# Start addresses of the MLP operands within 64 bytes, and one unread product ahead of the MLP's long run

## The chip, the cores and the metric

The kernel runs on one core of a Trainium2 chip. The metric is the device time of one execution in microseconds (us), lower is better. Three runs of the kernel before took 1395.46, 1397.22 and 1397.25 us, median 1397.22.

## The reference

Attention with mixed heads, and two MLPs behind it, all in float32. q, k and v are 4 x 12 x 448 x 64 (batch, heads, positions, width), the model width is 768, the inner width of both MLPs 2048:

```
scores = einsum('bhij,hg->bgij', q @ k^T / 8, w_pre)
attn   = softmax(scores)
attn   = einsum('bhij,hg->bgij', attn, w_post)
x      = (attn @ v), heads side by side            # 1792 x 768
x      = elu(x @ w_in) @ w_out                     # first MLP
out    = relu(x @ w_in2)**2 @ w_out2               # second MLP
```

## The kernel before

Every float32 operand of the scores, the pre mix and the MLPs is split into a high and a low part of type fp32r, and a product is three matmuls: high x high, high x low, low x high. In the MLPs the helper `three` issues them (lines 576 to 578). Its first two operands are the stationary ones, which a weight load brings into TensorE; the last two are the moving ones, which stream through it.

Attention runs in 90 steps of two row groups each. In a step come two pre mixes (lines 189 to 191, fp32r, 120 x 120 stationary, 448 columns moving), softmax, sometimes a set of scores (line 162) or of `values` (line 245, the product with v, in float32, 64 stationary columns, two halves of the array in turn), and then two post mixes (`mix_post`, line 220, float32, 112 stationary columns, 120 moving ones, two records on the engine for each matmul). Behind the last step the code calls `mlps.begin()`, which issues the first 36 MLP matmuls, and after it the last two `values`, which fill the wait for the last mixed rows. Then `run` issues the rest of the MLPs.

The 1792 rows go through the MLPs in two halves of 896, and each half in four stages:

- inner stage of the first MLP: 16 blocks of the inner width, two blocks of 448 rows, 6 steps of the sum, three matmuls each, 576 matmuls of 448 columns. Stationary is a weight (`wh`, `wl`), moving is `xh` or `xl`. In the first half the 36 of `begin` are part of it
- outer stage of the first MLP (w1o): 576 matmuls of 448 columns, stationary a weight, moving `hh` or `hl`
- inner stage of the second MLP: as the first
- outer stage of the second MLP (w2o): 672 matmuls of 384 columns. Here the roles change: stationary is `hh` or `hl`, moving is a weight

Each weight comes by a DMA as 64-bit numbers, is turned into float32 by one operation of ScalarE and four of VectorE (lines 430 to 454), and split (lines 467 and 468). The second half loads float32 weights that the first half kept.

Where the tiles lie: as built, within a partition, `xh` begins at byte 186336 and `xl` at 207840, the four buffers of `wh` at 148704 to 154848 and of `wl` at 156896 to 163040, all 32 bytes past a multiple of 64. `hh` and `hl` begin at 16512 and 73856, multiples of 64. All slices that `three` takes step by multiples of 256 bytes, so a stage has one start for each role:

| stage | stationary starts at (mod 64) | moving starts at (mod 64) |
|---|---|---|
| both inner stages | 32 | 32 |
| w1o | 32 | 0 |
| w2o | 0 | 32 |

Of the pre mix, `gh` and `gl` (moving) are at 0, `pre_l` at 0 and `pre_h` at 32. The tile `pre`, from which `pre_h` and `pre_l` are made, is at byte 16512, under what becomes `hh`.

The PSUM banks have three tags, `qk` with four buffers, `mix` and `post` with two each. The MLPs take them in the order mix, post, qk, qk (`Mlps.bank`).

Of the kernel before, what the change touches and what calls it, by code (L numbers as in the profile page):

```python
# [8 lines left out]
F32R = mybir.dt.float32r  # L9
# [6 lines left out]
B, H, S, D = 4, 12, 448, 64  # L16
# [4 lines left out]
JC, NJ = 4, 112  # L21
KC, FC = DM // 128, DFF // 128
WU = 512
EXP_MIN, EXP_MAX = 2.0**-15, float.fromhex("0x1.dffffep+16")


# [17 lines left out]
def bank(psum, tag):  # L44
    return psum.tile([128, 512], F32, name=f"ps_{tag}", tag=tag, bufs=BANKS[tag])


def attention(tc, psum, qr, kr, vr, w_pre, w_post, diagonal, xd, mlps):
    nc = tc.nc
    with ExitStack() as ctx:  # L50
# [339 lines left out]
        for i in range(2):  # L390
            values(N - 1, i)


class Weights:

# [5 lines left out]
    def __init__(self, nc, dram, layers):  # L401
        self.nc = nc
        self.units = []
        kept = [dram.tile([count, 128, n], F32, name=f"{name}f", tag=f"{name}f") for name, _, count, n in layers]
        for half in range(2):
            for k, (name, src, count, n) in zip(kept, layers):
                self.units += [(half, src[i], k[i], n) for i in range(count)]
        self.raw, self.single, self.parts, self.keep = {}, {}, {}, []
        self.loaded = self.sized = self.turned = self.done = self.used = 0

    def load(self, room=None):
        i = self.loaded
        self.loaded += 1
        half, src, kept, n = self.units[i]
        if half == 0:
            self.raw[i] = (room() if room else self.pool.tile([128, WU, 2], I32, name="wd", bufs=4))[:, :n, :]
            self.nc.sync.dma_start(out=self.raw[i].rearrange("p n t -> p (n t)"), in_=src.bitcast(I32))
        else:
            self.single[i] = self.pool.tile([128, WU], F32, name="wf", bufs=6)[:, :n]
            self.nc.sync.dma_start(out=self.single[i], in_=kept)  # L420

    def size(self, room=None):

        i = self.sized
        self.sized += 1
        half, src, kept, n = self.units[i]
        if half == 1:
            return
        f = (room() if room else self.pool.tile([128, WU], F32, name="wf", bufs=6))[:, :n]
        self.nc.scalar.activation(f, self.raw[i][:, :, 1].bitcast(F32), AF.Abs)  # L430
        self.single[i] = f
# [5 lines left out]
    def turn_op(self, k):  # L437

        nc = self.nc
        i = self.turned  # L440
        half, src, kept, n = self.units[i]
        if half == 0:
            if self.sized == i:
                self.size()
            t, f = self.raw[i], self.single[i]
            low, high, w = t[:, :, 0], t[:, :, 1], f.bitcast(I32)
            if k == 0:
                nc.vector.tensor_scalar(f, f, EXP_MIN, EXP_MAX, ALU.max, ALU.min)
            elif k == 1:
                nc.vector.tensor_scalar(w, w, 5, 2, ALU.logical_shift_left, ALU.logical_shift_right)  # L450
            elif k == 2:
                nc.vector.scalar_tensor_tensor(w, high, -0x40000000, w, ALU.bitwise_and, ALU.bitwise_or)
            else:
                nc.vector.scalar_tensor_tensor(w, low, 29, w, ALU.logical_shift_right, ALU.bitwise_or)  # L454
                del self.raw[i]
                self.keep.append((kept, f))
        self.turned += k == 3

    def part(self, engine=None):
        nc = self.nc  # L460
        i = self.done
        self.done += 1
        f = self.single.pop(i)
        n = self.units[i][3]
        hi = self.pool.tile([128, WU], F32R, name="wh", bufs=4)[:, :n]
        lo = self.pool.tile([128, WU], F32R, name="wl", bufs=4)[:, :n]
        nc.scalar.copy(hi, f)  # L467
        (engine or nc.vector).tensor_tensor(lo, f, hi.bitcast(F32), ALU.subtract)  # L468
        self.parts[i] = hi, lo
# [27 lines left out]
def col(i):  # L497
    return slice(i * 128, (i + 1) * 128)


class Mlps:
# [14 lines left out]
    def tmp(self):  # L516
        return self.tp.tile([128, S], F32, name="tmp", bufs=5)

    def two_parts(self, shape, pool, name):
        return [pool.tile(shape, F32R, name=f"{name}{a}", tag=f"{name}{a}") for a in "hl"]  # L520


    def plan(self, put, M, last, work, early, early_ctx, score_ctx):
# [29 lines left out]

    def new_x(self, half):
        self.half, self.xraw = half, {}
        self.nx = self.two_parts([128, KC, 2 * S], self.xp, "x")

    def piece(self, i):

# [37 lines left out]
    def run(self):  # L597
        nc, weights, blocks = self.nc, self.weights, self.blocks
        self.hp = self.pool("hp", "left")
        for half in range(2):  # L600
            xh, xl = self.nx
            for m in range(2):
                hh, hl = self.two_parts([128, FC, 2 * S], self.hp, "h")
                pending = []

                def activate(p, f, bl, m=m, hh=hh, hl=hl):
                    u = g = self.tmp()
                    if m == 0:
                        nc.scalar.activation(u, p, AF.Relu, scale=-1.0)
                        nc.scalar.activation(u, u, AF.Exp, scale=-1.0)  # L610
                        nc.vector.scalar_tensor_tensor(g, u, -1.0, p, ALU.add, ALU.max)
                    else:
                        nc.scalar.activation(u, p, AF.Relu)  # L613
                        nc.vector.tensor_tensor(g, u, u, ALU.mult)  # L614

                    def rest():
                        nc.scalar.copy(hh[:, f, bl], g)
                        nc.vector.tensor_tensor(hl[:, f, bl], g, hh[:, f, bl].bitcast(F32), ALU.subtract)

                    pending.append(rest)  # L620

                def flush():
                    for rest in pending:
                        rest()
                    pending.clear()

                for f in range(FC):
                    if half == m == f == 0:
                        p = self.begun
                    else:  # L630
                        p = self.inner(xh, xl, flush)
                    for j, bl in enumerate(blocks):
                        activate(p[j], f, bl)
                flush()
                if m == 0:
                    xh, xl = self.two_parts([128, KC, 2 * S], self.xp, "x")
                    for o in range(KC):
                        p = [self.bank()[:, :S] for _ in blocks]
                        for f4 in range(4):
                            wh, wl = weights.next()  # L640
                            for j, bl in enumerate(blocks):
                                for i in range(4):
                                    f = 4 * f4 + i
                                    self.three(p[j], wh[:, col(i)], wl[:, col(i)], hh[:, f, bl], hl[:, f, bl],
                                               f == 0, f == FC - 1)
                        for j, bl in enumerate(blocks):
                            nc.scalar.copy(xh[:, o, bl], p[j])
                            nc.vector.tensor_tensor(xl[:, o, bl], p[j], xh[:, o, bl].bitcast(F32), ALU.subtract)
                    continue
                n2 = DM // 2  # L650
                for nh in range(2):
                    p = [self.bank()[:, :n2] for _ in range(7)]
                    for f in range(FC):
                        if half == 0 and nh == 0:
                            if f == 0:
                                self.new_x(1)
                            if f < 12:
                                self.load_x(f)
                            if 2 <= f < 14:
                                self.split_x(f - 2)  # L660
                        wh, wl = weights.next()
                        for i in range(7):
                            self.three(p[i], hh[:, f, col(i)], hl[:, f, col(i)], wh[:, :n2], wl[:, :n2],
                                       f == 0, f == FC - 1)
                    for i in range(7):
                        o = self.tmp()[:, :n2]
                        if i % 2:
                            nc.scalar.copy(o, p[i])
                        else:
                            nc.vector.tensor_copy(o, p[i])  # L670
                        r = half * 2 * S + i * 128
                        nc.sync.dma_start(out=self.out[r : r + 128, nh * n2 : (nh + 1) * n2], in_=o)
# [49 lines left out]
```

## Time and profile before

| | us |
|---|---|
| median of three runs | 1397.22 |
| the profiled execution | 1395.56 |
| its span, first to last instruction | 1393.8 |
| attention, up to the first matmul behind the last values | 445.9 |
| MLPs from there to the last matmul's start | 944.1 |

The profile is one execution on the one core. TensorE has two rows, PE for the matmuls and PEld for the weight loads, which run beside them; DVE is VectorE, ACT ScalarE, POOL GpSimd. A matmul's record is longer than its share of the engine, since the next one starts before it ends: what counts is the pitch, from the start of one to the start of the next. Where the pitch is even, a record of an MLP matmul is some 161 to 164 ns longer than it.

### The profile page before, as it was taken

What the parts mean: (1) busy time and instruction counts of PE and PEld (TensorE: products, weight loads), DVE (VectorE), ACT (ScalarE), POOL (GpSimd) and SP (SyncE); (2) the same over time, 40 slices, a digit from 0 to 9 for tenths busy, and PEclk for the clock granted to TensorE, in tenths of its full rate; (3) what the DMA queues carried; (4) which work ended last, traced back from release to release, by engine and by line L of the source; (5) the groups of instructions that cost most, each with busy time, mean ns of one, the idle gap of its engine ahead of it and who ended that gap; (6) DMA issues with size and microseconds to landing.
All of it is one profiled execution on the core that took longest, in us unless ns stands there. A gap on an engine that the chain in (4) does not pass through costs nothing.

```text
span 1393.8 us, 24193 instructions
## 1 busy us (share of the span) xinstructions
PE 1381.4 (99%) x8906; PEld 1249.7 (90%) x8906; DVE 859.0 (62%) x1928; ACT 669.6 (48%) x1504; POOL 263.4 (19%) x245
## 2 busy tenths in 40 slices
PE   7999999999999999999999999999999999999999
PEld 4888888888889999999999999999999999999998
DVE  6877778777886989766688886534442114443121
ACT  5776767676775666322354543245541113333111
POOL 3755665665554000000000000000000000000000
PEclk9999999999999999999999999999999999999999
DMA  5624633734544555544455575431221111111131
GB/s 157 198 105 146 192 106 131 205 107 130 192 137 158 180 159 177 189 148 144 143 163 154 166 253 186 150 100 54 61 68 53 46 46 46 57 56 57 36 108 40
DMA packets 104810, 174.40 MB, mean 125 GB/s; under 512 B 22675, under 2 KB 82163, under 8 KB 104691
## 3 DMA queue, kind: packets, MB, share of 16 engines
q1 hardware_dynamic: 104691, 172.85, 39.4%
q8 instruction: 70, 1.15, 0.3%
q14 instruction: 49, 0.40, 0.1%
HBM read 97.93 MB, written 36.18 MB: 96 GB/s over the span
## 4 chain that ended last, share of the span: by engine, by line
PE 98%; DVE 1%; ACT 0%; DMA 0%; issue 0%; POOL 0%; SPq 0%; DVEq 0%
PE ps_post L220 12%; PE ps_qk L576 11%; PE ps_qk L577 11%; PE ps_qk L578 11%; PE ps_mix L577 6%; PE ps_post L577 6%; PE ps_mix L576 6%; PE ps_post L576 6%; PE ps_post L578 6%; PE ps_mix L578 6%; PE ps_qk L245 6%; PE ps_qk L162 4%; PE ps_mix L191 3%; PE ps_mix L190 2%; PE ps_mix L189 2%; DMA k_room<-kr 0%
## 5 line engine op out<-in xcount | busy, mean ns | idle before, releaser
L467 ACT CAST wh<-wf 128x384 fp32r<-128x384 f32 (+1 forms) x240 | 126.6, 532 | 272.4 <-DVE wf L454 113.8
L468 DVE TENSOR_TENSOR wl<-wf,wh 128x384 fp32r<-128x384 f32 (+1 forms) x238 | 137.3, 581 | 163.2 <-ACT wh L467 162.3
L183 POOL TENSOR_TENSOR gl<-graw,gh 120x448 fp32r<-120x448 f32 x178 | 201.5, 1154 | 145.7 <-ACT gh L178 142.4
L220 PEld LDWEIGHTS ps_post<-wg,ex 120*112 120x112 f32 x1440 | 156.1, 177 | 21.6 <-DVE tot L204 7.5
L220 PE MATMUL ps_post<-wg,ex 120*112 120x120 f32 x1440 | 172.9, 272 | 0.7 <-DVE at L227 0.6
L198 ACT ACTIVATE ex<-ps_mix,nmax 120x448 f32<-120x448 f32 x180 | 113.5, 637 | 113.5 <-DVE nmax L196 110.2
L576 PE MATMUL ps_qk<-xh,wh 128*128 128x448 f32 x384 | 141.4, 368 | 0.0
L577 PE MATMUL ps_qk<-xl,wh 128*128 128x448 f32 x384 | 141.3, 368 | 0.0
L578 PE MATMUL ps_qk<-xh,wl 128*128 128x448 f32 x384 | 141.3, 368 | 0.0
L196 DVE TENSOR_REDUCE nmax<-ps_mix 120x1 f32<-120x448 f32 x180 | 109.6, 622 | 41.7 <-PE ps_mix L191 41.3
L227 DVE COPY at<-ps_post 112x480 f32<-112x480 f32 x162 | 105.4, 650 | 9.9 <-PE ps_post L220 9.9
L178 ACT CAST gh<-graw 120x448 fp32r<-120x448 f32 x180 | 95.2, 593 | 0.1
L614 DVE TENSOR_TENSOR tmp<-tmp 128x448 f32<-128x448 f32 x64 | 39.9, 623 | 77.6 <-ACT tmp L613 77.6
L165 ACT COPY sc<-ps_qk 120x448 f32<-120x448 f32 x178 | 82.2, 558 | 7.1 <-PE ps_qk L162 7.0
L245 PEld LDWEIGHTS ps_qk<-at,v 112*64 112x64 f32 x1536 | 73.8, 137 | 11.3 <-ACT gh L178 6.5
L245 PE MATMUL ps_qk<-at,v 112*64 112x110 f32 (+2 forms) x1536 | 81.8, 262 | 0.0
L576 PEld LDWEIGHTS ps_qk<-xh,wh 128*128 128x128 f32 x384 | 72.1, 188 | 7.3
L577 PEld LDWEIGHTS ps_qk<-xl,wh 128*128 128x128 f32 x384 | 72.1, 188 | 7.3
L578 PEld LDWEIGHTS ps_qk<-xh,wl 128*128 128x128 f32 x384 | 72.1, 188 | 7.2
L430 ACT ACTIVATE wf<-wd 128x384 f32<-128x384 f32 (+1 forms) x120 | 69.4, 578 | 18.0 <-DMA wd<-w2o 8.6
L577 PE MATMUL ps_qk<-wl,hh 128*128 128x384 f32 x224 | 75.9, 339 | 0.0
L576 PE MATMUL ps_qk<-wh,hh 128*128 128x384 f32 x224 | 75.8, 339 | 0.0
(137 smaller groups left out, 3155.4 us busy)
## 6 DMA issues: line engine op xcount, KB each, us to landing
graw<-sc SPq DMA_DIRECT2D x180, 210.0 KB
wd<-w1i SPq DMA_DIRECT2D x32, 384.0 KB
wd<-w1o SPq DMA_DIRECT2D x24, 512.0 KB
wd<-w2i SPq DMA_DIRECT2D x32, 384.0 KB
wd<-w2o SPq DMA_DIRECT2D x32, 384.0 KB
w1if<-wf SPq DMA_DIRECT2D x32, 192.0 KB
w1of<-wf SPq DMA_DIRECT2D x24, 256.0 KB
w2if<-wf SPq DMA_DIRECT2D x32, 192.0 KB
```

The lines of the kernel that those rows point to most:

```text
L178: nc.scalar.copy(hi, graw[t])
L183: engine.tensor_tensor(lo, graw.pop(t), parts[t][0].bitcast(F32), ALU.subtract)
L196: nc.vector.tensor_reduce(nmax, p, AX.X, ALU.max, negate=True)
L198: nc.scalar.activation(e[-1], p, AF.Exp, bias=nmax, scale=1.0, accum_out=tot[:, t % 2 : t % 2 + 1])
L220: nc.tensor.matmul(p[:, c, :], e[:, c * NJ : (c + 1) * NJ], w, start=True, stop=True)
L227: nc.vector.tensor_copy(o, p)
L245: nc.tensor.matmul(p[64 * a : 64 * a + 64, k, :w], vt[b, i][:, jc, g * D : (g + 1) * D], at[n][:, jc, 6 * i + g, :w], start=(jc == 0), sto ...
L467: nc.scalar.copy(hi, f)
L468: (engine or nc.vector).tensor_tensor(lo, f, hi.bitcast(F32), ALU.subtract)
L576: mm(p, wh, xh, start=first, stop=False)
L577: mm(p, wh, xl, start=False, stop=False)
L578: mm(p, wl, xh, start=False, stop=last)
```

## The change

There are two parts.

1. Start addresses. The tiles of `xh`, `xl`, `hh` and `hl` become 16 elements (64 bytes) longer, and what is used of them begins `at` elements in: 8 (32 bytes) for x, 0 for the hidden values of the first MLP, 8 for those of the second. The weights of w2o begin 8 elements into their tiles, all others at 0 as before. Worked out from the tile sizes, the x pool grows down from the same top by 128 bytes, so `xh`'s tile stays at 32 past a multiple of 64 and its used part comes to a multiple of 64; the weight tiles move down by 128 bytes and stay at 32; `hh` stays at 16512 and `hl` comes to 73920. So in every stage of the MLPs the moving operands begin at a multiple of 64 bytes and the stationary ones 32 past one.
2. Behind the last `values` one more matmul is issued: the first 112 columns of `pre` stationary, all its 120 columns moving, float32, into a bank of tag `post`. Nothing reads the result.

```
+OFF = 8
         for i in range(2):
             values(N - 1, i)

+        flat = pre.rearrange("p r g -> p (r g)")
+        nc.tensor.matmul(bank(psum, "post")[:NJ, :120], flat[:, :NJ], flat, start=True, stop=True)
...
-                self.units += [(half, src[i], k[i], n) for i in range(count)]
+                self.units += [(half, src[i], k[i], n, name == "w2o") for i in range(count)]
...
-        hi = self.pool.tile([128, WU], F32R, name="wh", bufs=4)[:, :n]
-        lo = self.pool.tile([128, WU], F32R, name="wl", bufs=4)[:, :n]
+        at = OFF * self.units[i][4]
+        hi = self.pool.tile([128, WU], F32R, name="wh", bufs=4)[:, at : at + n]
+        lo = self.pool.tile([128, WU], F32R, name="wl", bufs=4)[:, at : at + n]
...
-    def two_parts(self, shape, pool, name):
-        return [pool.tile(shape, F32R, name=f"{name}{a}", tag=f"{name}{a}") for a in "hl"]
+    def two_parts(self, k, pool, name, at):
+
+        n = k * 2 * S
+        t = [pool.tile([128, n + 2 * OFF], F32R, name=f"{name}{a}", tag=f"{name}{a}") for a in "hl"]
+        return [x[:, at : at + n].rearrange("p (k s) -> p k s", k=k) for x in t]
...
-        self.nx = self.two_parts([128, KC, 2 * S], self.xp, "x")
+        self.nx = self.two_parts(KC, self.xp, "x", OFF)
...
-                hh, hl = self.two_parts([128, FC, 2 * S], self.hp, "h")
+                hh, hl = self.two_parts(FC, self.hp, "h", m * OFF)
...
-                    xh, xl = self.two_parts([128, KC, 2 * S], self.xp, "x")
+                    xh, xl = self.two_parts(KC, self.xp, "x", OFF)
```

## Rows read from the trace of the kernel before

**Rows 1.** The page: span, busy time of PE, the chain that ended last

```profile
span 1393.8 us, 24193 instructions
...
PE 1381.4 (99%) x8906; PEld 1249.7 (90%) x8906; DVE 859.0 (62%) x1928; ACT 669.6 (48%) x1504; POOL 263.4 (19%) x245
...
PE 98%; DVE 1%; ACT 0%; DMA 0%; issue 0%; POOL 0%; SPq 0%; DVEq 0%
```

**Rows 2.** Stretches, PE alone: start:end us, length, busy (records), clock, DMA

```profile
434.72:440.80 6.08, 6.08 (x32) 1.00 0.27 78
446.61:557.59 110.98, 110.98 (x538) 1.00 0.56 180
557.59:676.62 119.03, 119.03 (x577) 1.00 0.49 160
676.62:795.65 119.03, 119.03 (x577) 1.00 0.50 157
795.65:914.38 118.73, 118.73 (x674) 1.00 0.57 184
914.38:1033.41 119.03, 119.03 (x578) 1.00 0.24 72
```

**Rows 3.** Timeline of PE around the 36 early MLP matmuls: start us, us, what

```profile
431.26 0.97 PE L245 MATMUL ps_qk<-at,v 112*64 112x110 f32 x16
432.17 1.89 PE L220 MATMUL ps_post<-wg,ex 120*112 120x120 f32 x16
433.82 0.45 PE L576 MATMUL ps_mix<-xh,wh 128*128 128x448 f32 x1
434.11 0.36 PE L577 MATMUL ps_mix<-xl,wh 128*128 128x448 f32 x1
...
434.72 0.36 PE L577 MATMUL ps_mix<-xl,wh 128*128 128x448 f32 x1
...
440.80 0.36 PE L577 MATMUL ps_post<-xl,wh 128*128 128x448 f32 x1
```

**Rows 4.** Timeline of PE behind the last values

```profile
445.60 0.35 PE L245 MATMUL ps_qk<-at,v 112*64 112x108 f32 x4
445.89 0.47 PE L576 MATMUL ps_qk<-xh,wh 128*128 128x448 f32 x1
446.20 0.36 PE L577 MATMUL ps_qk<-xl,wh 128*128 128x448 f32 x1
446.40 0.37 PE L578 MATMUL ps_qk<-xh,wl 128*128 128x448 f32 x1
446.61 0.37 PE L576 MATMUL ps_qk<-xh,wh 128*128 128x448 f32 x1
```

**Rows 5.** Matmuls on tile hh: ns min/median/max, first and last start

```profile
L576 PE MATMUL ps_qk<-wh,hh x224: 336/338/342, 796.7 to 1389.7; 128*128 128x384 f32 x112
```

**Rows 6.** Timeline of PE, the last two pre mixes

```profile
427.09 0.36 PE L189 MATMUL ps_mix<-gh,pre_l 120*120 120x448 f32 x1
427.28 0.36 PE L190 MATMUL ps_mix<-gh,pre_h 120*120 120x448 f32 x1
427.48 0.37 PE L191 MATMUL ps_mix<-gl,pre_h 120*120 120x448 f32 x1
```

**Rows 7.** Timelines of DVE, PE and ACT: readers of the banks, first write of hh

```profile
434.10 0.53 DVE L229 COPY at<-ps_post 112x360 f32<-112x360 f32 x1 [0.29 <-PE ps_post L220]
...
448.68 0.61 DVE L611 SCALAR_TENSOR_TENSOR tmp<-tmp,ps_post 128x448 f32<-128x448 f32 x1
...
455.29 0.37 PE L576 MATMUL ps_post<-xh,wh 128*128 128x448 f32 x1
...
449.41 1.03 ACT L617 CAST hh<-tmp 128x448 fp32r<-128x448 f32 x2
```

**Rows 8.** Stretches, all engines: PE, PEld, DVE, ACT, POOL busy (records), clock, DMA

```profile
460.00:550.00 90.00, 90.00 (x437) 81.74 (x437) 83.01 (x176) 62.12 (x124) 0.00 (x0) 1.00 0.54 167
```

More of the change, by code (lines that the diff above doesn't have):

```diff
@@ L413, in load @@
         self.loaded += 1
-        half, src, kept, n = self.units[i]
+        half, src, kept, n, moves = self.units[i]
         if half == 0:
@@ L425, in size @@
         self.sized += 1
-        half, src, kept, n = self.units[i]
+        half, src, kept, n, moves = self.units[i]
         if half == 1:
@@ L440, in turn_op @@
         i = self.turned
-        half, src, kept, n = self.units[i]
+        half, src, kept, n, moves = self.units[i]
         if half == 0:
```

## The prediction

> **What bounds the kernel now.** I began with the busy times and the chain of waits on the page: TensorE's matmul row is busy 1381.4 of 1393.8 us, and 98% of the chain that ended last is its own matmuls [rows 1]. So no other engine, queue or transfer counts unless it starves TensorE. Next I cut the MLPs into their stages and asked for TensorE's busy time in each: it fills every stretch without a gap, at full granted clock, which of the two levels is 2.4 GHz [rows 2]. What is left to look at is how long a matmul occupies the engine, its pitch. The bounds of the stretches are starts of matmuls, so length over count is the pitch:
>
> - inner stage of the first half, from the fourth matmul behind the last values: 110.98 us / 537 = 206.67 ns [rows 2]
> - w1o: 119.03 / 576 = 206.65 ns, and the same for the next inner stage and for the first one of the second half [rows 2]
> - w2o, 384 columns: 118.73 / 672 = 176.68 ns [rows 2]
>
> Then I read the start of the MLPs one matmul at a time, because there the same matmuls stand behind two different neighbours. The 36 early ones follow a post mix. From the fifth to the thirty-fifth, 30 pitches, they take 6.08 us, 202.67 ns each [rows 2, 3]. Behind the last values the same kind of matmul, on the same tiles and weight buffers, falls within three matmuls to 206.67 and stays there for 537 in a row [rows 2, 4]. Operands, shapes, clock and addresses mod 64 are alike, so 4.0 ns a matmul hang on something that the engine carries over from what ran before it. It is carried far: w2o has another pitch for 672 matmuls, and the inner stage behind it is at 206.65 again [rows 2]. The trace shows that this is so, not what it is. I call the two the short and the long rhythm.
>
> **The change part by part.** *The unread product* puts something like a post mix where the values now lead straight into the long run. The trace has that order once: values until 432.17, post mixes, then the early matmuls in the short rhythm [rows 3]. There the post mix made 16 records; the new product makes 2. If two are enough, all 448-column matmuls behind it run at 202.67: 540 of the first inner stage less the 3 that lead in, 576 of the next two stages, 3 x 576 of the second half, say 3420. That is 3420 x (206.67 - 202.67) = 13.7 us saved, all of it on the chain, as TensorE has no gaps. For w2o, whose pitch in the short rhythm no row shows, I take no change; its records spread from 336 to 342 ns [rows 5], so single pitches lie about 3 ns on either side of the mean, and 1344 matmuls at 3 ns would be 4.0 us either way.
>
> The product itself costs its own time. Now the first MLP matmul starts behind the last values and the second 0.31 us later [rows 4]. With a product between, two records of some 0.10 to 0.19 us (16 in 1.89 us with the first wait in it) precede it, and the first fp32r matmul behind a post mix has a pitch of 0.29 instead of 0.31 [rows 3, 4]. I charge 0.2 us; 0 and 0.4 are the ends.
>
> What it could wait for: the bank of tag `post` that it takes was last read by the copy of the last mixed rows, at 434.10 to 434.63 [rows 7], 11 us before. What could wait for it: the tag's two buffers change parity, so the next MLP block on a `post` bank, at 455.29, now takes the buffer whose last reader ends at 449.29 [rows 7]; 6 us cover it. The tile `pre` lives until the product has read it, and `hh` lies over it, but the first write of `hh` is at 449.41, more than 3 us after the values that it waits for anyway [rows 7]; no more than 0.2 us could come back there, in ScalarE's queue, with the weights' casts behind it. I cost all three at nothing.
>
> *The start addresses* add no instruction, wait or byte of transfer; the moves of the pools by 128 bytes put no tile over a neighbour that it did not lie over before. They touch two of the four stages in what the engine sees as relative start: inner stages go from 32/32 (stationary/moving, mod 64) to 32/0, w2o from 0/32 to 32/0. w1o has 32/0 already, and there the pitch in the long rhythm is the same 206.65 as with 32/32 [rows 2]. So in the long rhythm the new addresses are worth nothing for 448 columns. In the short rhythm 32/0 is only seen in the pre mixes, which have loads of 120 columns and no more than six in a row: 0.19 and 0.20 us, about 196 and 200 ns [rows 6]. With loads of 128 columns it will be somewhat more. The nearest row in kind is the early stretch, 202.67, and I take it for the new addresses too, that is 0 for this part. Its ends: 196 as in the shortest pre mix, which is 6.7 x 3456 = 23 us more saved, and 206.67, which takes the whole gain back.
>
> Beside TensorE only VectorE comes near: in the first inner stage it is busy 83.0 of 90 us [rows 8], 92%. At 202.67 the stage is 2% shorter and VectorE at 94%; at 196 it would be 97%. So it starves nothing before the low end.
>
> The Trainium skill has a rule against the address part: TensorE: Matmul & The Clock Gate, Step-by-step: what each phase is for, says that the moving operand and the weight load have independent read ports, so that loading the next weights takes no read bandwidth from the running matmul. By it no start address would matter, and this part would be worth exactly nothing. The equal pitch of w1o and the inner stages agrees; the two rhythms of one and the same matmul are nothing that it explains.
>
> Sum against the profiled execution: 1395.6 - 13.7 + 0.2 = 1382.1 us. That execution is 1.7 us under the median of the runs shown, so against the median 1397.2 - 13.5 = 1383.7, say 1384.
>
> **The rivals.**
>
> *Nothing moves.* The long rhythm comes back at once, because two records don't do what 16 did, or because it hangs on the phase in which the first fp32r matmul happens to start; or the first change of stage brings it back (540 x 4.0 = 2.2 us saved). For it: the trace has only one start in the short rhythm, of 36 matmuls. Against it: within that stretch nothing drifts, and the long rhythm outlives three changes of stage. 1395 to 1397.5.
>
> *Lost half way.* The short rhythm holds in the first half and is lost at w2o: (540 + 1152) x 4.0 = 6.8 us, 1390.5. Against it speaks that the long rhythm outlives w2o.
>
> *The addresses bring more than the rhythm.* With 32/0 in the short rhythm the pitch goes to that of the shorter pre mixes: between 196 and 199.5 for 448 columns, and w2o to the lower edge of its records, 3 ns less. At 198: (206.67 - 198) x 3420 + 3 x 1344 + 0.2 = 29.7 + 4.0 = 34 us, 1363; at 196 it is 1357. For it: the pre mixes are the only rows with this pairing and have the lowest pitches. Against it: loads of 120 columns, runs of six.
>
> *Slower: w2o takes w1o's pairing and with it its evenness.* w1o, with 32/0, has one single pitch and it is the long one; w2o, with 0/32, varies, and only its longest matmuls reach 342 ns, 4 ns over the median of 338 [rows 5]. If the long rhythm stays and 32/0 makes each of the 1344 as long as the longest, w2o's pitch becomes about 180: 1344 x 3.3 = 4.5 us, with the product 1402. It decides from a rise of 2.1 ns in w2o's mean, if the other stages keep theirs.
>
> TensorE: Matmul & The Clock Gate, Back-to-back issue gap, in the Trainium skill gives a floor for a matmul by itself, columns / 2.4 GHz + 2.5 ns. An estimate from it: 189.2 ns for 448 columns and 162.5 for 384, 79 us in all, 1318; no stretch of the MLPs comes near it, and I give it 1 in 100, inside the chance of the rival that the addresses bring more.
>
> **How the numbers follow.** Chances: forecast 0.52 (1376 to 1389 with w2o's 4 us, the product's ends and 1 ns on the pitch); addresses bring more 0.15; lost half way 0.07; nothing moves 0.16; slower 0.10. A measurement of this kernel can tell 0.2%, 2.8 us, from no change. Forecast, the larger gain and the half-way case are faster: 0.74. Same: 0.16. Slower: 0.10. The range of 8 in 10 leaves out the slower case and about a third of the larger gain: 1360 to 1399.
>
> **What would show each step.** Right: a stretch of the first inner stage of the changed kernel has a pitch near 202.7 in uneven single pitches, w1o too, and the first inner stage of the second half still has it. The product shows as two records of line 220's kind of length behind the last values and TensorE has no gap after it. Wrong: an even 206.67 behind the product (two records are not enough, or the phase decides); a change of pitch in the inner stages but not in w1o, which has no new addresses (then it is the addresses, not the rhythm); w2o even at 180; or a pitch under 200 everywhere, by which the addresses would be worth more than the rhythm. A wait of TensorE for `wl` in the first inner stage would mean that VectorE has become the bound.

## The result, and the profile after

The changed kernel takes 1380.59 us (median of 4 runs, 1380.01 to 1381.63), the kernel before in the same comparison 1396.43 us. The ratio is 0.9888, 95% interval 0.9875 to 0.9900: 1.1% faster. The forecast was 1384 us, range 1360 to 1399. Size and direction came out; the cause that I gave for it did not, as the experiments show.

The page of the changed kernel answers to [rows 1]: TensorE is still busy all the time, only for less of it.

```profile
span 1378.3 us, 24196 instructions
...
PE 1366.5 (99%) x8908; PEld 1247.3 (90%) x8908; DVE 859.0 (62%) x1928; ACT 669.5 (49%) x1504; POOL 263.4 (19%) x245
...
PE 97%; DVE 1%; ACT 0%; issue 0%; DMA 0%; POOL 0%; SPq 0%; ACTq 0%; DVEq 0%; POOLq 0%
```

VectorE and ScalarE do the same work in the same busy time as before. The stretches of TensorE by stage (start:end us, length, busy and records, clock, DMA share, GB/s), which answer to [rows 2]; each runs from the start of a matmul to that of another:

```profile
446.90:556.09 109.19, 109.19 (x538) 1.00 0.57 182
556.09:673.21 117.12, 117.12 (x577) 1.00 0.51 163
673.21:790.33 117.12, 117.12 (x577) 1.00 0.50 159
790.33:906.83 116.50, 116.50 (x673) 1.00 0.58 188
906.83:1023.95 117.12, 117.12 (x577) 1.00 0.24 73
```

Length over matmuls: 109.19 / 537 and 117.12 / 576 are 203.33 ns in every 448-column stage, inner or w1o alike, where it was 206.67. 116.50 / 672 is 173.4 ns for w2o (the first few matmuls of it are longer; from the ninth on 173.33), where it was 176.68. The sum: 3420 x 3.33 ns = 11.4 us and 1344 x 3.33 ns = 4.5 us, less 0.3 us for the later start of the long run, 15.6 us. The two profiled executions differ by 1395.56 - 1380.11 = 15.5 us. So nothing is hidden elsewhere: the whole change is in the pitch.

The timeline of TensorE behind the last values (start us, us, what), answering to [rows 4]:

```profile
445.97 0.46 PE L395 MATMUL ps_post<-pre 120*112 120x120 f32 x2
446.19 0.45 PE L584 MATMUL ps_qk<-xh,wh 128*128 128x448 f32 x1
446.48 0.37 PE L585 MATMUL ps_qk<-xl,wh 128*128 128x448 f32 x1
446.68 0.38 PE L586 MATMUL ps_qk<-xh,wl 128*128 128x448 f32 x1
446.90 0.37 PE L584 MATMUL ps_qk<-xh,wh 128*128 128x448 f32 x1
```

The product is there with its two records. The first MLP matmul moves from 445.89 to 446.19; 0.22 us of that lie between the start of the product and it, the rest was there before the product.

One thing already spoke against my reading: the 36 early matmuls, which I took as the model for what a post mix does, ran at 202.67 ns before and run at 203.33 now. The fifth and the thirty-fifth of them:

```profile
434.77 0.37 PE L585 MATMUL ps_mix<-xl,wh 128*128 128x448 f32 x1
...
440.88 0.37 PE L585 MATMUL ps_post<-xl,wh 128*128 128x448 f32 x1
```

That is 6.11 us for 30 pitches (6.10 before the rows are rounded), where it was 6.08. The common pitch of all 448-column stages is not that of the short rhythm; it is a third value. It is only 0.3% above 202.67, so my own sign of being right, a pitch near 202.7 in every stage, could not tell the two apart.

### The profile page after: what moved, and what is told of

Its sections match the earlier page's. It is cut to its first block, busy times and chain, and to the rows that moved or that the text cites. A ratio compares the mean times of both kernels' runs of the same rounds, so it can differ in the third digit from the quotient of the medians.

```text
span 1378.3 us, 24196 instructions
## 1 busy us (share of the span) xinstructions
PE 1366.5 (99%) x8908; PEld 1247.3 (90%) x8908; DVE 859.0 (62%) x1928; ACT 669.5 (49%) x1504; POOL 263.4 (19%) x245
## 4 chain that ended last, share of the span: by engine, by line
PE 97%; DVE 1%; ACT 0%; issue 0%; DMA 0%; POOL 0%; SPq 0%; ACTq 0%; DVEq 0%; POOLq 0%
PE ps_post L221 12%; PE ps_qk L585 11%; PE ps_qk L586 11%; PE ps_qk L584 11%; PE ps_qk L246 6%; PE ps_mix L585 6%; PE ps_post L585 6%; PE ps_post L586 6%; PE ps_mix L586 6%; PE ps_mix L584 6%; PE ps_post L584 6%; PE ps_qk L163 4%; PE ps_mix L192 3%; PE ps_mix L190 3%; PE ps_mix L191 3%
```

## The experiments

### One part at a time: the product alone, the addresses alone

The product alone, on the kernel before:

```
         for i in range(2):
             values(N - 1, i)
+        flat = pre.rearrange("p r g -> p (r g)")
+        nc.tensor.matmul(bank(psum, "post")[:NJ, :120], flat[:, :NJ], flat, start=True, stop=True)
```

> The kernel before with the unread product alone; all start addresses as before (32/32 in the inner stages, 32/0 in w1o, 0/32 in w2o, stationary/moving mod 64). Theory A, the product resets a carried state and the addresses add a second, separate gain: the inner stages run at 202.7 ns as the early 36, uneven; w2o is near its 176.7 or up to 3 ns under; total 1381 to 1385 us. Rival B, the addresses do it all: 206.67 behind the product and 176.67 in w2o, 1396 us. Rival C, only both together do it: as B.

Measured: 1396.03 us (10 runs, 1395.80 to 1397.14), ratio 0.9999, interval 0.9990 to 1.0008. Its stretches, w1o, the second inner stage and w2o of the first half:

```profile
557.82:676.86 119.04, 119.04 (x578) 1.00 0.49 160
676.86:795.89 119.03, 119.03 (x578) 1.00 0.50 156
795.89:914.61 118.72, 118.72 (x673) 1.00 0.58 184
```

These are the pitches of before: 206.67, 206.65 and 176.67 ns. The long run starts 0.25 us later, and that is all. Theory A, on which the forecast's 13.7 us rested, falls.

The addresses alone (the changed kernel without those two lines):

```
-        flat = pre.rearrange("p r g -> p (r g)")
-        nc.tensor.matmul(bank(psum, "post")[:NJ, :120], flat[:, :NJ], flat, start=True, stop=True)
```

> The changed kernel without the product: new start addresses, 32/0 in all stages. Theory A: the long rhythm stays, 206.67 in all 448-column stages as w1o had with this pairing before; w2o, which gets that pairing, between 173.3 and 180; total 1391 to 1401 us. Rival B: the pitch is 203.33 and 173.33 as in the changed kernel, 1380 us.

Measured: 1381.33 us (4 runs, 1380.66 to 1381.64), ratio 0.9891, interval 0.9874 to 0.9907; the whole change has 0.9888, so no difference is to be seen. The same three stages:

```profile
557.62:674.74 117.12, 117.12 (x577) 1.00 0.50 163
674.74:791.86 117.12, 117.12 (x578) 1.00 0.50 159
791.86:908.36 116.50, 116.50 (x674) 1.00 0.58 188
```

203.33, 203.33 and 173.4 ns: rival B, to the digit. The start addresses make the whole gain, in all four stages, w1o included, although mod 64 nothing changed there.

### Are there two rhythms, and what decides between them?

The kernel before had shown one matmul at two pitches. If not one product, what moves it? First, one product in another place, ahead of w1o of the first half:

```
                 if m == 0:
+                    if half == 0:
+                        f32 = xh[:120, 0, :120].bitcast(F32)
+                        nc.tensor.matmul(self.bank()[:NJ, :120], f32[:, :NJ], f32, start=True, stop=True)
                     xh, xl = self.two_parts([128, KC, 2 * S], self.xp, "x")
```

> The kernel before with one unread float32 product (112 stationary columns, 120 moving, from the bits of xh) issued not behind the last values but between the first inner stage and w1o of the first half. If a float32 product with over 64 stationary columns sets a state that lasts: the first inner stage at 206.67, and w1o and both later inner stages at 202 to 204, about 1386 us. If it is the phase in which the long run starts, or something that only the values leave behind and that the first matmuls wash into a fixed rhythm: no change at w1o, 1395 us.

Measured, one run: 1382.42 us. The first inner stage, w1o, the second inner stage, w2o, and the first inner stage of the second half:

```profile
447.74:558.85 111.11, 111.11 (x540) 1.00 0.56 180
559.13:674.14 115.01, 115.01 (x576) 1.00 0.50 164
674.14:790.88 116.74, 116.74 (x577) 1.00 0.51 159
790.88:909.60 118.72, 118.72 (x673) 1.00 0.57 185
909.60:1026.34 116.74, 116.74 (x578) 1.00 0.25 73
```

Up to the product the pitch was 206.67 (the first row less the 0.34 us around the product at its end, 110.77 us for 536 pitches). From it on w1o runs at 200.0 ns and the inner stages at 202.67 (116.74 / 576), and that is kept across w2o, whose own pitch, 176.67, is the same in both cases. So with the old addresses there are two rhythms, and they can outlast a change of stage: this much of my reading stands. That the product made the change is not shown by one execution; it also takes a bank, so all later blocks use the banks in another order. Then two products behind the last values in place of one (`for _ in range(2):` ahead of the matmul):

> The kernel before with two unread products behind the last values, four records in place of two. If the product resets a state: the same pitches as with one product, stage by stage, and 0.2 us more. If the phase at the start decides: the pitch may fall back to 206.67 or come out as a third value.

Measured, one run: 1381.32 us, the first inner stage, w1o and the second inner stage:

```profile
449.04:557.87 108.83, 108.83 (x538) 1.00 0.57 180
557.87:673.09 115.22, 115.22 (x577) 1.00 0.51 166
673.09:789.83 116.74, 116.74 (x577) 1.00 0.51 159
```

In this execution two products were followed by the short rhythm, 202.67 and 200.0 ns, where one was followed by the long one. The long run also began later, at 448.35 instead of 446.14 us, of which the second product explains 0.5; so the number of products is not told apart from the moment of the start. One product with 112 moving columns in place of 120 (`flat[:, :NJ]` as the moving operand too):

> The kernel before with one unread product of 112 moving columns where prod_only had 120; the same two records, stationary columns and bank. If the phase at which the run of MLP matmuls starts decides between the two rhythms, some 16 clock cycles less may give the short one, 202.7 and 200.0 in w1o, about 1382 us. If one product is too little to reset a state, 206.67 as with 120 columns, 1396 us.

Measured, one run: 1396.10 us; its w1o is at 206.67 ns:

```profile
558.12:677.16 119.04, 119.04 (x578) 1.00 0.49 160
```

One product behind the last values left the long rhythm, with 120 columns in ten executions and with 112 in one; one product ahead of w1o was followed by the short one, in one execution. If a program can come out either way, single executions decide nothing here. Three products, timed twelve times:

> The kernel before with three unread products behind the last values, old start addresses, timed many times for how the executions spread. If four records or more set a state that two don't: the short rhythm in every execution, 202.7 in the inner stages and 200.0 in w1o, about 1381.5 us. If the instant at which the run of MLP matmuls begins decides, against something that the program doesn't set: either class may come out, 1381 or 1396.5 us, and executions of one program may differ, as one untouched execution of the kernel before came at 1380.53 among others at 1395.6 to 1397.5.

Measured: 1384.64 us median, and the executions fall in two groups: ten at 1383.87 to 1385.75, two at 1396.76 and 1397.98. The kernel before, in the same comparison, fell in two groups as well: eleven at 1395.42 to 1397.10, five at 1379.05 to 1380.41. Within each group of runs the program is the same in all executions. The profiled one of three products shows even a mixture: the first inner stage, w1o of the first half, the second inner stage, and w1o of the second half:

```profile
448.08:556.91 108.83, 108.83 (x538) 1.00 0.57 180
556.91:675.95 119.04, 119.04 (x577) 1.00 0.50 161
675.95:792.70 116.75, 116.75 (x577) 1.00 0.51 159
1028.15:1143.35 115.20, 115.20 (x577) 1.00 0.17 51
```

202.66, 206.67, 202.69 and 200.0 ns: w1o in the long rhythm between two inner stages in the short one, and in the short one itself half a pass later. So a rhythm can change at the boundary of a stage with no product there, which may also be what happened in the run with the product ahead of w1o. And the program alone doesn't settle the rhythm; the counts suggest that it shifts the odds: in this comparison 2 of 12 executions with three products were in the upper group, against 11 of 16 of the kernel before. Over all comparisons 6 of 42 executions of the kernel before were under 1381 us. None of those six was profiled; that they are the short rhythm is concluded from their time, which is within 2.3 us of the one with two products. What stands ahead does seem to weigh: in all six profiled runs with the old addresses the 36 early matmuls, behind the post mixes, are in the short rhythm, 6.08 us for 30 pitches, whatever the long run shows later.

### How much of an address counts

In the changed kernel `hl` and `xl` begin 64 bytes off `hh` and `xh`, mod 128, because each tile grew by 64 bytes. Growing by 128 instead leaves everything mod 64 as the change has it:

```
-        t = [pool.tile([128, n + 2 * OFF], F32R, name=f"{name}{a}", tag=f"{name}{a}") for a in "hl"]
+        t = [pool.tile([128, n + 32], F32R, name=f"{name}{a}", tag=f"{name}{a}") for a in "hl"]
```

> The changed kernel with its x and hidden tiles longer by 128 bytes in place of 64, so that the high and the low tile of a pair start at the same place mod 128 (in the changed kernel they are 64 apart); mod 64 nothing changes. Theory D, the gain of the changed kernel comes from the two parts of an operand lying 64 bytes apart mod 128, which puts every run between the two rhythms whatever came before (203.33 is the mean of 206.67 and 200.0): here all 448-column stages are bimodal again, 206.67 (1395 us or somewhat under it by w2o) or 200.0 (1370 us). Rival E, only the place mod 64 counts, as the change's words have it: 203.33 and 173.33 as in the changed kernel, 1380 us.

> The same with two unread products in place of one. Theory D: the class of the rhythm follows the start; with two products, which gave the short one with the old addresses, all 448-column stages run at 200.0 as w1o did there, w2o at 173 to 177: 1368 to 1374 us. Rival E: 203.33 and 173.33, 1380 us.

Measured, one run each: 1388.93 us with one product, 1388.54 with two. w1o and w2o with one product:

```profile
558.79:676.55 117.76, 117.76 (x577) 1.00 0.49 162
794.31:912.28 117.97, 117.97 (x673) 1.00 0.58 186
```

204.44 ns and 175.55 ns, and the same to 0.02 ns with two products. Neither theory had that. "A multiple of 64 and 32 past it" holds here in every stage, and much of the gain is gone: by the pitches 3420 x 2.23 + 1344 x 1.12 ns = 9.1 us are left of 15.9. The measured gain is smaller, 6.9 us, since in this execution the long run began 2.4 us later than in the kernel before:

```profile
448.31 0.45 PE L584 MATMUL ps_qk<-xh,wh 128*128 128x448 f32 x1
```

That start lies between 445.89 and 448.35 us in the profiled runs, and no run shows why; kernels timed once are better compared by their pitches. So the place mod 64 does not describe what counts. And two rhythms are not to be seen, in the few executions at hand, where the two parts of an operand lie apart.

A scan followed, with other distances in each stage (weights and hidden tiles begin at `at` elements that differ by layer and half), on that kernel with two products. Its distances are taken from the moving start to the stationary one, stationary less moving, mod 128:

```
+                at = {"w1i": (16, 24), "w1o": (0, 0), "w2i": (4, 12), "w2o": (8, 8)}[name][half]
...
-                hh, hl = self.two_parts(FC, self.hp, "h", m * OFF)
+                hh, hl = self.two_parts(FC, self.hp, "h", ((16, 8), (8, 24))[half][m])
```

> The kernel with 128 bytes of padding and two products, with another distance from moving to stationary start (mod 128 bytes, high and low alike) in each stage: first half inner 32, w1o 32, second inner 112, w2o 32; second half inner 64, w1o 64, inner 16, w2o 96. If the distance mod 64 is what counts, distance 32 gives 200.0 as 96 did, and 64 the 202.7 of distance 0; if mod 128, 32 and 64 come out otherwise. 112 and 16 are blind: a lower pitch than 200.0 at any distance would be a way to a faster kernel. Total 1365 to 1395 us.

Measured, one run: 1381.98 us. The first inner stage, w1o, the second inner stage and w2o of the first half, and w1o and w2o of the second:

```profile
448.64:558.41 109.77, 109.77 (x538) 1.00 0.56 180
558.41:676.17 117.76, 117.76 (x577) 1.00 0.50 162
676.17:792.65 116.48, 116.48 (x577) 1.00 0.51 160
792.65:910.63 117.98, 117.98 (x673) 1.00 0.58 186
1027.10:1143.58 116.48, 116.48 (x578) 1.00 0.17 50
1260.06:1376.38 116.32, 116.32 (x673) 1.00 0.19 57
```

The 448-column stages come out at 204.44 (distances 32, both the inner stage and w1o) and 202.2 (112, 64, 64 and 16); w2o at 175.57 and 173.35. That the two inner stages and w1o agree where the distance agrees, whichever of the two starts was moved, is the first sign that the distance is what counts. But 32 is 204.44 here, and 96 was 200.0 or 206.67 in w1o of the kernel before, so it is not mod 64. It is not mod 128 either: in the run with longer tiles both parts of every 448-column stage had 96 mod 128, as w1o has in the kernel before, and ran at 204.44. Taken mod 256 the high and the low parts of that kernel have different distances, 128 apart, and all stages so far sort by the pair.

The next scan has both parts at one place mod 256, so that each stage has one distance d, now and from here on the other way round (start of the moving operand less start of the stationary one, mod 256):

```
+                at = {"w1i": (56, 32), "w1o": (0, 0), "w2i": (40, 8), "w2o": (0, 16)}[name][half]
...
+        t = [pool.tile([128, n + 64 * (name == "h")], F32R, name=f"{name}{a}", tag=f"{name}{a}") for a in "hl"]
...
+                hh, hl = self.two_parts(FC, self.hp, "h", ((40, 16), (8, 0))[half][m])
...
+                    xh, xl = self.two_parts(KC, self.xp, "x", 0)
```

> Two products, and in every stage the high and the low part of each operand at the same place mod 256 bytes, so that all three matmuls of a product have one and the same distance from stationary to moving start. Distances (moving minus stationary, mod 256): first half inner 32, w1o 64, second inner 96, w2o 32; second half inner 128, w1o 192, second inner 224, w2o 160. Theory F, the pitch goes by this distance mod 256, since all stages so far sort by it (0: 206.67 or 202.67; 160: 206.67 or 200.0; the mixed pairs 32 and 96: 203.33, 32 and 160 or 96 and 224: 204.44, 64 and 192 or 16 and 144: 202.22): each stage gets a pitch of its own, and one of them is under 200.0 for 448 columns, most likely where the moving start is shortly ahead of the stationary one (32 or 64). Rival, the distance counts mod 64 alone: 32, 96, 160 and 224 are all alike and like w1o before (200.0 in the class of two products), 64, 128 and 192 like 0 (202.67).

Measured, one run: 1380.90 us. Its stages in order, d = 32, 64, 96, (w2o) 32, 128, 192, 224, (w2o) 160:

```profile
447.51:557.30 109.79, 109.79 (x539) 1.00 0.57 179
557.30:672.50 115.20, 115.20 (x578) 1.00 0.51 166
672.50:790.77 118.27, 118.27 (x578) 1.00 0.51 158
790.77:907.25 116.48, 116.48 (x673) 1.00 0.59 188
907.25:1024.74 117.49, 117.49 (x577) 1.00 0.25 73
1024.74:1141.22 116.48, 116.48 (x577) 1.00 0.18 50
1141.22:1258.98 117.76, 117.76 (x578) 1.00 0.19 54
1258.98:1375.28 116.30, 116.30 (x672) 1.00 0.19 57
```

| d mod 256 | 448 columns, ns | seen in |
|---|---|---|
| 0 | 206.67 or 202.67 | inner stages of before, the kernels with products |
| 32 | 204.45 (the 36 early ones 206.67) | this run |
| 64 | 200.00 | this run |
| 96 | 205.33 | this run |
| 128 | 203.98 | this run |
| 160 | 206.67 or 200.00 | w1o of before, the kernels with products |
| 192 | 202.22 | this run |
| 224 | 204.44 | this run |

Distances that are alike mod 64 (64, 128, 192) differ by up to 4 ns, so the rival falls. Theory F stands as a sorting and fails in its bet: nothing is under 200.0, and 32 is no good place, 64 is. It is also not the distance alone, since 0, 32 and 160 have each shown two values. Nor do the distances of a product's three matmuls average: the changed kernel mixes 32 and 96 and has 203.33 ns, less than this run has at 32 (204.45) or at 96 (205.33).

### A kernel made from the table

d = 64 in all 448-column stages, 32 in w2o, without and with products, the tiles as in the last scan:

```
+                at = {"w1i": (48, 48), "w1o": (0, 0), "w2i": (48, 48), "w2o": (0, 0)}[name][half]
...
+                hh, hl = self.two_parts(FC, self.hp, "h", ((40, 16), (40, 16))[half][m])
```

> Start addresses by the sorting so far: in every 448-column stage the moving start lies 64 bytes (mod 256) ahead of the stationary one for all three matmuls of a product, in w2o 32; no unread product. Theory F, the distance mod 256 sets the pitch: 200.0 in all 448-column stages and 173.33 in w2o, 1369 to 1371 us. Rival G, 200.0 at distance 64 was seen in one stage of one run only and hangs on the class of the start: here, without a product, 204 to 207, 1380 to 1395 us.

> The same with two unread products behind the last values, as in the run that showed 200.0 at distance 64. Theory F: as without them, 1369 to 1371 us. Rival G: 200.0 here and something longer without the products.

Measured: 1371.34 us without a product (4 runs, 1370.61 to 1372.14), 1372.46 with two (4 runs, 1371.92 to 1372.70). The ratios to the kernel before are 0.9840 (0.9786 to 0.9894) and 0.9848 (0.9784 to 0.9913); the intervals are wide because one of the seven executions of the kernel before, at 1380.53 us, falls into the lower group. w1o and w2o of the first half and w2o of the second, without a product:

```profile
555.21:670.42 115.21, 115.21 (x578) 1.00 0.51 166
785.63:902.11 116.48, 116.48 (x674) 1.00 0.59 188
1247.72:1366.26 118.54, 118.54 (x672) 1.00 0.18 56
```

and with two:

```profile
555.27:670.47 115.20, 115.20 (x577) 1.00 0.52 167
785.68:904.39 118.71, 118.71 (x673) 1.00 0.58 185
1250.02:1366.32 116.30, 116.30 (x672) 1.00 0.19 57
```

Every 448-column stage of both is at 200.0 ns, the 36 early matmuls too: theory F, and rival G falls. w2o at d = 32 has two rhythms, 173.33 and 176.66, and each run shows one in each half, the other way round; so theory F misses for w2o, and both times lie a little above its 1369 to 1371. The kernel without a product is 24 us under the kernel before (median 1395.70 in this comparison), 9 us under the change (1380.59 in another comparison), and 8 to 9 us under the lower group of the kernel before. At d = 64 the inner stages were brought there by moving the weights and w1o by moving the hidden values, and both have 200.0: this is the best evidence here that the distance counts and not a place by itself.

## Why the prediction was right, and where it was not

*The bound.* Right: the chain is TensorE's, its pitch is all that changed, and no engine, wait or transfer took any of it back. VectorE's share in the first inner stage rose from 92% to 94% (84.2 of 90 us) and starved nothing.

*The unread product, 13.7 us.* Wrong, and it was the step that carried the sum. The product alone gives a ratio of 0.9999 and the old pitch in every stage. I had one instance of the short rhythm behind a post mix, read it as "a post mix resets the engine", and asked only whether two records would be enough. The runs show two rhythms that can last, as I said; but what a program puts ahead shifts the odds at most. The kernel before falls into two groups itself, 16 us apart, from one execution to another. The rival that nothing moves, at 0.16, had this part right; its reason, the phase in which the first fp32r matmul happens to start, is not shown either, since with three products the rhythm changed twice after the start.

*Its own cost, 0.2 us, and the three covers at nothing.* Right: from the product's start to the first MLP matmul it is 0.22 us; the long run starts 0.25 us later with the product alone, 0.3 in the changed kernel, and TensorE has no gap after it.

*The start addresses, 0 for 448 columns and for w2o.* Wrong: they are everything, 3.33 ns on each matmul of either kind, 15.9 us. The argument was that w1o has the change's pairing already and the same pitch as the inner stages. It was made mod 64, as the change is worded; mod 256 w1o stood at 160 before and at 32 and 96 after. The ends for 448 columns, 196 and 206.67, hold the measured 203.33; the 3 ns for w2o were a little short of its 3.3. The rival that the addresses bring more had the sign of this part right and its size too large: 198 or 196 ns, 1363 or 1357 us.

*w2o.* The slower rival had 180 ns for it; it came to 173.33, near the lower end of its single pitches.

*Two sums.* The rival that the addresses bring more adds the product's 0.2 us to the gain where it should take it off, and the forecast's upper end comes to 1391 by its own three terms, not 1389. Neither decides anything.

The number came out by luck: two errors nearly cancelled, 13.7 us that the product didn't bring, and 15.9 that the addresses did. And it hides a point: the gain is over an execution in the long rhythm. The short one has 202.67, 200.0 and 176.67 ns where the change has 203.33, 203.33 and 173.33, and the executions taken for it, 1379.05 to 1380.53 us, are no slower than the change's 1380.01 to 1381.63. What the change does is to take the draw away, as far as eight executions show: the four each of the change and of the addresses alone were all within 1.7 us.

## What to carry to other kernels

Where TensorE is full, measure the pitch of one matmul stage by stage, and take a difference between equal matmuls as something to gain; then do each part of a change alone, since one row that looks like cause and effect may be chance. Start addresses of moving and stationary operands are a parameter worth a scan: it costs no instruction, several distances fit in one execution if each stage has its own, and here it was worth 1.7% of a kernel that had no gap left (0.6% against its executions near 1380 us). Time a kernel often enough to see whether its executions form two groups before comparing medians.

## What the runs showed of the hardware

- The pitch of an fp32r matmul of 448 columns with a weight load of 128 beside it lies between 200.0 and 206.67 ns at the full granted clock, and where it lies goes with the start of the moving operand less that of the stationary one, mod 256 bytes, for the high and the low part together; of the distances in the table all but 0, 64 and 160 were seen in one execution each. At 384 columns it was 173.33 to 176.67.
- For some distances there are two stable rhythms (0: 206.67 and 202.67; 160: 206.67 and 200.0; w2o at 32: 176.66 and 173.33). One can last for all 3420 448-column matmuls of the long run, as the long one does in the profiled execution of the kernel before, or change from one stage to the next, as with three products; by their times, executions of one program come in either. At 64, and where the high and the low part had different distances, each 448-column stage showed one value only, whatever came before.
- The Trainium skill, TensorE: Matmul & The Clock Gate, Step-by-step: what each phase is for, says that loading the next tile's weights takes no SBUF read bandwidth from the running matmul. Read strictly, that leaves the start of the one against the start of the other nothing to act on. Here the addresses alone moved every pitch by 3.33 ns and, at distance 64, those of 448 columns by 6.67, both against the long rhythm; the measurement decides, though it does not show what the two share.

What stays open: the mechanism. No run here shows whether anything collides, and what, why 64 is good and 32 not, or what at the start of a run decides between two rhythms; the table is a sorting of one or a few executions for each distance, in steps of 32 bytes; steps of 16 were seen only in the first scan, at 16 and 112 as it counts them.
